# Twelve phases to a unit by a table, and the maxima taken together one pair later

## The chip, the cores and the metric

The kernel runs on one core of a Trainium2 chip. A core has a matrix engine (TensorE, "PE" in the profile, with its weight loads shown apart as "PEld"), a vector engine (VectorE, "DVE"), an engine for elementwise functions (ScalarE, "ACT"), a general engine (GpSimd, "POOL") and an engine that here only issues transfers (SyncE, "SP"). Each takes its own instructions in order and waits on semaphores for the others. TensorE writes to PSUM, a buffer of eight banks of 2 KB per partition, from where VectorE and ScalarE read. The metric is the device time of one execution in microseconds.

## The reference

Four layers on `x` of 2048 rows and 576 columns, in the order A, B, A, B. Each is an attention block of 32 heads of width 18 behind a layer norm, with a residual:

```python
def _A_ref(x, wqkv, wo):                     # B: one k and one v shared by all heads
    q, k, v = ...                            # x @ wqkv, 32 heads of 18
    scores = jnp.einsum("bhqd,bhkd->bhqk", q, k) * (Dh ** -0.5)
    p = _softmax(scores, axis=-1)
    o = jnp.einsum("bhqk,bhkd->bhqd", p, v)
    return (...)(o, 0, 2, 1, 3).reshape(B, S, D) @ wo

x = x + _A_ref(_layernorm(x), A_wqkv, A_wo)  # then B, A, B in the same way
```

Everything is fp32. Softmax is over 2048 keys, for 32 heads times 2048 queries, in each layer.

## The kernel before

Heads are worked in pairs (`NPAIR` = 16), and queries in four quarters of 512. A **unit** is one pair of heads and one quarter of queries, `(p, u)`; there are 64 in a layer. Operands of head 0 of a pair lie on partitions 0 to 63 and those of head 1 on 64 to 127, so that a matmul of one head uses one half of TensorE's rows. A unit has three kinds of matmul:

- **Products for the maxima** (`max_mm`, "m", L506): 128 queries against 512 keys of one head; 32 to a unit. Two of them fill the two banks of a tile `psm` (two such tiles, four banks). VectorE reduces a full tile along the keys (`reduce_max`, L515). After 32 products `max_final` (L626) takes the maxima of the unit together and negates them; GpSimd splits them into a high and a low part (L139, L630). `max_store` (L635, L637) transposes them on VectorE and stores them to DRAM in four transfers; `max_rows` (L641) loads them as two rows of the query operand.
- **Products for the exps** (`exp_mm`, "e", L650): 128 keys against 512 queries of one head, with the negated maximum in the two added rows; 32 to a unit. Each goes to one of three banks, `pse`; ScalarE turns it into a tile `pt` of probabilities (L654).
- **Products with the values** (`pv_cols`, `pv_block`, L675): four `pt` tiles at a time, each with 19 columns of weights (18 values and a one that gives the sum), in four column groups of TensorE. They add up in one bank, `oacc`. 4096 columns to a unit, eight blocks of 512. When a unit's last block is done, ScalarE copies the bank (L681).

The products for the maxima run ahead of those for the exps by 56 (`4 * LEAD`), the value products follow the exps two phases later. GpSimd then sums the parts, inverts the sums and scales (`o_sum`, `l_inv`, `o_mul`), with transfers between. Such work is entered in a table by steps of four exps (`at`, `run_todo`), and `run_todo` emits what has come due at the beginning of a phase.

The order of the work on TensorE is written out. The loop at L764 runs **phases**: row products, m and e, in an order given by `ORDERS`, then a number of value columns. A unit has eleven phases. Those with an even number have two m and three e, those with an odd number four m and three e, the eleventh two of each. The heads of the m alternate with the phase, the exps come in a fixed order (two of head 0, two of head 1). Ten phases have 384 value columns, the eleventh 256:

```python
for kind, n in ORDERS[2 if k == 10 else k % 2]:
    if kind == "e":
        ...exp_mm(...)
    elif m_done[0] < 4 * ns:
        max_mm(n ^ k // 2 % 2, ...)
exps += 2 if k == 10 else 3
if phase >= 2:
    pv_cols(256 if k == 10 else 384)
```

In `max_mm`, the reduce of the unit's last pair is followed at once by `max_final`. When all m are done, the same loop goes on with the e and the value columns that are left. At the beginning of a layer, m products alone are woven into the projections (`max_pairs`).

Of the kernel before, what the change touches and what calls it, by code (L numbers as in the profile page):

```python
# [19 lines left out]
NCH = S // P  # L20
NPAIR = H // 2
# [21 lines left out]
STEPS = 8  # L43
LEAD = 14
# [14 lines left out]

ORDERS = ([("m", 1), ("e", 0), ("m", 1), ("e", 1), ("e", 2)],
          [("m", 0), ("m", 1), ("e", 1), ("e", 0), ("m", 0), ("m", 1), ("e", 2)],
          [("m", 1), ("e", 0), ("m", 1), ("e", 1)])


@with_exitstack
def tile_kernel(ctx: ExitStack, tc: tile.TileContext, A_x, A_wqkv, A_wo, B_x, B_wq, B_wk, B_wv, B_wo, out):
# [53 lines left out]
    def mtile2(name):  # L123
        return psum.tile([P, 2, 512], F32, tag="m", bufs=2, name=name)
# [7 lines left out]
    def ptile(name, shape=(P, 512), dt=F32):  # L132
        return pool.tile(list(shape), dt, tag="p", bufs=15, name=name)

    def copy(eng, dst, src):
        if eng is nc.scalar:
            eng.activation(dst, src, AF.Copy)  # L137
        else:
            eng.tensor_scalar(dst, src, 1.0, 0.0, op0=OP.mult, op1=OP.add)  # L139
# [194 lines left out]
    def out_proj(last):  # L334

        for c in range(NCH):
            tt = c // 2
            if c == 1:
                out_rows(2)
            if c % 2 and tt + 3 < 8:  # L340
                out_rows(tt + 3)
            if c >= OUT_AHEAD:
                run_tail(TAIL)
            out_w(c)
            if c % 2 == 0 and tt + 1 < 8:
                out_t(tt + 1, nc.scalar)
            if last:
                nc.sync.dma_start(y_out[c * P:(c + 1) * P, :], xo[:, c])
            yield c
        assert not tail and not ors  # L350
# [4 lines left out]
    for layer in range(4):  # L355
# [124 lines left out]
        def ops(p):  # L480
            return big[:, q_slot(p)], big[:, k_slot(p)]

        m_open, m_next, m_done, m_count = [], [0, 0], [0], {}

        m_first = [] if is_a else ([(0, i // 2, i % 2) for i in range(8)] + [(1, i // 2, i % 2) for i in range(4)] +
                                   [(0, i, 2) for i in range(4)] + [(1, i // 2, i % 2) for i in range(4, 6)] +
                                   [(0, i, 3) for i in range(4)] + [(1, i // 2, i % 2) for i in range(6, 8)] +
                                   [(1, i, 2) for i in range(4)] + [(1, i, 3) for i in range(4)])

        def max_mm(a, slot):  # L490

            i = m_next[a]
            p, u = divmod(i // 16, 4)
            if i < len(m_first):
                u, qc, kb = m_first[i]
            else:
                qc, kb = i // 2 % 4, i // 8 % 2 * 2 + i % 2
            q, k = ops(p)
            if (p, u) not in mxs:
                mxs[p, u] = pool.tile([P, 32], F32, name="mx")  # L500
            if m_done[0] % 2 == 0:
                m_open.append((mtile2("psm"), []))
            ps, rows = m_open[0]
            b = 64 * a
            c0 = u * 512 + qc * P
            nc.tensor.matmul(ps[:, slot], q[b:b + KM, c0:c0 + P], k[b:b + KM, kb * 512:(kb + 1) * 512],  # L506
                             start=True, stop=True)
            rows.append((p, u, 16 * a + 4 * qc + kb))
            m_next[a] += 1
            m_done[0] += 1  # L510
            if m_done[0] % 2 == 0:
                m_open.pop()
                (p, u, r0), (p1, u1, r1) = sorted(rows)
                assert (p, u) == (p1, u1)
                nc.vector.reduce_max(mxs[p, u][:, r0:r1 + 1:r1 - r0], ps, axis=AX.X)  # L515
                m_count[p, u] = m_count.get((p, u), 0) + 2
                if m_count[p, u] == 32:
                    max_final(p, u)

        def max_pairs():  # L520

            if is_a:
                run_todo(m_done[0] // 4)
            for a in (0, 1, 0, 1):
                max_mm(a, a)
            if not is_a and m_done[0] == 48:
                max_store(0, 0)
            elif not is_a and m_done[0] == 52:
                max_rows(0, 0)
# [94 lines left out]
        def max_final(p, u):  # L624
            neg = pool.tile([P, 8], F32, name="neg")
            nc.vector.tensor_reduce(neg, mxs.pop((p, u)).rearrange("p (b k) -> p b k", k=4), axis=AX.X, op=OP.max,  # L626
                                    negate=True)
            hl = nms[p, u] = hls[(4 * p + u) % 2]
            copy(nc.gpsimd, hl[:, 0:8], neg)
            nc.gpsimd.tensor_tensor(hl[:, 8:16], neg, hl.bitcast(F32)[:, 0:8], op=OP.subtract)  # L630

        def max_store(p, u):

            tr = pool.tile([P, 32], F32, name="tr")
            nc.vector.transpose(tr, nms.pop((p, u)).bitcast(F32))  # L635
            for b in range(4):
                nc.sync.dma_start(m_d[u].rearrange("j a q (b i) -> b (j a q) i", b=4)[b], tr[32 * b:32 * b + 16, :])  # L637

        def max_rows(p, u):
            for a in range(2):  # L640
                nc.sync.dma_start(big_f[64 * a + KM:64 * a + KE, q_slot(p), u * 512:(u + 1) * 512],  # L641
                                  m_d[u][:, a].rearrange("j q p -> j (q p)"))

        def exp_mm(p, u, i, tail):

            a, kc = (i // 2) % 2, i // 4 * 2 + i % 2
            q, k = ops(p)
            e = (mtile if tail and i % 2 else etile)("pse")
            r = 64 * a
            nc.tensor.matmul(e, k[r:r + KE, kc * P:(kc + 1) * P], q[r:r + KE, u * 512:(u + 1) * 512],  # L650
                             start=True, stop=True)

            pt = pts[p, u, i] = ptile("pt")
            nc.scalar.activation(pt, e, AF.Exp, scale=SCALE)  # L654

        turn, pv_at = [0], [0]

        def pv_cols(cols):

            while cols:  # L660
                n, c0 = divmod(pv_at[0], 512)
                w = min(cols, 512 - c0)
                pv_block(n, c0, c0 + w)
                pv_at[0] += w
                cols -= w

        def pv_block(n, c0, c1):

            p, u, i = *divmod(n // STEPS, 4), n % STEPS * 4
            cs = slice(c0, c1)  # L670
            turn[0] += 1
            for i in range(i, i + 4) if turn[0] % 2 else range(i + 3, i - 1, -1):
                a, kc = (i // 2) % 2, i // 4 * 2 + i % 2
                j = 64 * a + 32 * (kc % 2)
                nc.tensor.matmul(oacc[j:j + DH + 1, cs], v_of(kc)[:, 2 * p + a if is_a else 0, :], pts[p, u, i][:, cs],  # L675
                                 start=kc < 2 and c0 == 0, stop=kc >= 14 and c1 == 512)
                if c1 == 512:
                    pts.pop((p, u, i))
            if c1 == 512 and i // 4 == STEPS - 1:
                oc = ocs[p, u] = ptile("oc")  # L680
                nc.scalar.activation(oc, oacc, AF.Copy)  # L681
# [38 lines left out]
        def at(b, f, *args):  # L720
            todo.setdefault(b, []).append((f, args))

        ns = STEPS * 4 * NPAIR
        for p in range(NPAIR):
            for u in range(4):
                b = STEPS * (4 * p + u) + STEPS - 1
# [20 lines left out]
        def run_todo(st):  # L747
            for n in sorted(n for n in todo if n <= st):
                for f, args in todo.pop(n):
                    f(*args)  # L750
# [9 lines left out]
                woven(max_pairs, 3, 8)  # L760
            f(*args)
        assert not weave["left"] and m_done[0] == 4 * LEAD
        exps = 0
        for phase in range(11 * 4 * NPAIR):  # L764
            k = phase % 11
            run_todo(LEAD + exps // 4)
            for kind, n in ORDERS[2 if k == 10 else k % 2]:
                if kind == "e":
                    n += exps
                    exp_mm(*divmod(n // 4 // STEPS, 4), n % (4 * STEPS), m_done[0] >= 4 * ns)  # L770
                elif m_done[0] < 4 * ns:
                    max_mm(n ^ k // 2 % 2, m_done[0] % 2 if k % 2 == 0 else n ^ k // 2 % 2)
            exps += 2 if k == 10 else 3
            if phase >= 2:
                pv_cols(256 if k == 10 else 384)
        outs = out_proj(layer == 3)
        for st in range(ns, ns + L_AT + 1):
            run_todo(LEAD + st)
            if st < ns + OUT_AHEAD:
                next(outs)  # L780
                pv_cols(256 * (1 + st - ns))
        tail = [todo.pop(n, []) for n in range(ns + LEAD + L_AT + 1, ns + LEAD + O_AT)]
        assert not todo, todo

# [30 lines left out]
```

## Time and profile before

| | |
|---|---|
| median of three runs | 5806.96 us (5803.63 to 5808.14) |
| profiled execution | 5805.73 us, its span 5803.9 us |
| granted TensorE clock in it, mean | 0.997 |
| PE busy | 5767.2 us (99%) |
| DVE busy | 5170.2 us (89%) |
| ACT busy | 4605.2 us (79%) |
| POOL busy | 1718.2 us (30%) |
| mean DMA | 48 GB/s |

An engine's busy time is the union of its instructions' spans. Matmuls are pipelined and their ends are modelled, so 99% for PE does not say that the array is always fed: a wait of less than a matmul's tail does not show as idle time. What PE waited for is read on the row of its weight loads, and the length of a piece of work from the starts of its matmuls. In a group's line, the numbers after the bar are the busy time in us and the mean length of one in ns, and after the second bar the idle time just before them and what ended it. In a line of the timeline, the first number is the start and the second the length, both in us.

### The profile page before, as it was taken

How to read it: one execution, taken by the hardware profiler on the slowest of the kernel's cores; microseconds unless marked ns; L12 is line 12 of the kernel's file. 1: busy time of each engine (PE TensorE's matmuls, PEld its weight loads, DVE VectorE, ACT ScalarE, POOL GpSimd, SP SyncE). 2: the span in 40 equal slices, each digit the busy share in tenths (PEclk: the TensorE clock that was granted, in tenths of full speed). 3: DMA queues.
4: the chain of work that ended last, by engine and by line, in shares of the span. 5: the costliest groups of instructions: out<-in, count | busy, mean ns of one | idle time of the engine just before them, and what ended most of it. 6: DMA issues, size and time to landing. Idle time of an engine off the chain costs nothing.

```text
span 5803.9 us, 132703 instructions
## 1 busy us (share of the span) xinstructions
PE 5767.2 (99%) x53756; PEld 2906.5 (50%) x53756; DVE 5170.2 (89%) x5336; ACT 4605.2 (79%) x8872; POOL 1718.2 (30%) x2207
## 2 busy tenths in 40 slices
PE   9999999999999999999999999999999999999999
PEld 7644444444844444444685444444448444444446
DVE  4799999998699999999647999999977999999995
ACT  2588888888378888888625888888882888888885
POOL 2133232323233232323311423232332332323232
PEclk9999999999999999999999999999999999999999
DMA  5311111110420000000243111111114100010002
GB/s 195 110 46 31 36 31 35 32 32 21 127 65 23 22 22 20 20 22 24 59 166 93 40 35 32 35 32 35 29 35 128 49 22 23 22 23 19 23 13 77
DMA packets 250305, 276.40 MB, mean 48 GB/s; under 512 B 131732, under 2 KB 171924, under 8 KB 239972
## 3 DMA queue, kind: packets, MB, share of 16 engines
q1 hardware_dynamic: 249692, 267.92, 16.7%
q8 instruction: 422, 6.91, 0.5%
q14 instruction: 191, 1.56, 0.1%
HBM read 151.24 MB, written 112.56 MB: 45 GB/s over the span
## 4 chain that ended last, share of the span: by engine, by line
PE 97%; DVE 1%; DMA 1%; POOL 1%; ACT 0%; SPq 0%; issue 0%; POOLq 0%; ACTq 0%; DVEq 0%
PE oacc L675 36%; PE psm L506 31%; PE pse L650 17%; PE psn L215 6%; PE psq L374 6%; DVE mx L515 1%; PE ps L207 0%; DMA raw<-in_B_wk_dram 0%; ACT pt L654 0%; DMA big<-m_d 0%; POOL big L162 0%; PE oacc L208 0%; SPq L151 0%; POOL os L689 0%; POOL os L711 0%
## 5 line engine op out<-in xcount | busy, mean ns | idle before, releaser
L515 DVE TENSOR_REDUCE mx<-psm 128x2 f32<-128x1024 f32 x4096 | 4768.8, 1217 | 168.3 <-PE psm L506 133.6
L654 ACT ACTIVATE pt<-pse 128x512 f32<-128x512 f32 x8192 | 4314.4, 602 | 550.3 <-PE pse L650 368.2
L650 PE MATMUL pse<-big 64*128 64x512 f32 x8192 | 2448.6, 418 | 10.3 <-DMA big<-m_d 8.8
L506 PE MATMUL psm<-big 62*128 62x512 f32 x8192 | 2285.6, 452 | 5.7 <-DVE mx L515 5.6
L675 PE MATMUL oacc<-pt,vbuf 128*19 128x384 f32 (+1 forms) x24560 | 1756.0, 384 | 1.9 <-ACT oc L681 1.9
L506 PEld LDWEIGHTS psm<-big 62*128 62x128 f32 x8192 | 925.0, 184 | 1468.0 <-DVE mx L515 923.8
L650 PEld LDWEIGHTS pse<-big 64*128 64x128 f32 x8192 | 1188.3, 185 | 293.0 <-ACT pt L654 193.1
L675 PEld LDWEIGHTS oacc<-pt,vbuf 128*19 128x19 f32 x24560 | 501.0, 97 | 772.0 <-issue 594.3
L139 POOL TENSOR_SCALAR hl<-neg 128x8 fp32r<-128x8 f32 x256 | 50.9, 199 | 2681.0 <-DVE neg L626 2681.0
L675 PE MATMUL oacc<-pt,vy 128*19 128x256 f32 x8176 | 593.2, 385 | 0.0
L698 POOL TENSOR_TENSOR rl<-lt,mone 128x8 f32<-128x8 f32 x256 | 423.4, 1654 | 573.2 <-DMA lt<-os 573.1
L139 POOL TENSOR_SCALAR os<-oc 32x512 f32<-32x512 f32 x512 | 314.6, 614 | 129.6 <-ACT oc L681 87.7
L711 POOL TENSOR_TENSOR os<-os,rb 96x512 f32<-96x512 f32 x256 | 329.2, 1286 | 20.9 <-DMA rb<-r_d 20.1
L689 POOL TENSOR_TENSOR os<-os,oc 96x512 f32<-96x512 f32 x256 | 326.4, 1275 | 21.4
L382 ACT ACTIVATE ev<-psq 128x512 fp32r<-128x512 f32 (+1 forms) x112 | 67.0, 598 | 321.2 <-PE psq L374 240.4
L215 PE MATMUL psn<-wsm,xx 128*128 128x288 f32 x2240 | 307.4, 296 | 0.0
L215 PEld LDWEIGHTS psn<-wsm,xx 128*128 128x128 f32 x2240 | 298.6, 188 | 10.8 <-issue 8.0
L675 PEld LDWEIGHTS oacc<-pt,vy 128*19 128x19 f32 x8176 | 177.2, 98 | 251.1 <-issue 202.5
L388 DVE TENSOR_TENSOR ev<-psq,ev 128x512 fp32r<-128x512 f32 (+1 forms) x84 | 58.0, 691 | 218.6 <-ACT ev L382 202.9
L374 PE MATMUL psq<-yx,big 128*128 128x512 f32 (+2 forms) x812 | 199.6, 399 | 2.1 <-ACT big L137 0.8
L374 PE MATMUL psq<-xx,big 128*128 128x512 f32 (+1 forms) x784 | 194.5, 398 | 0.0
L681 ACT ACTIVATE oc<-oacc 128x512 f32<-128x512 f32 x256 | 157.7, 616 | 28.7 <-PE oacc L675 28.7
(66 smaller groups left out, 1370.9 us busy)
## 6 DMA issues: line engine op xcount, KB each, us to landing
big<-qk_d SPq DMA_DIRECT2D x180, 432.0 KB
qk_d<-ev SPq DMA_DIRECT2D x96, 512.0 KB
qk_d<-ev SPq DMA_DIRECT2D x120, 256.0 KB
rb<-r_d SPq DMA_DIRECT2D x512, 36.0 KB
o_d<-os SPq DMA_DIRECT2D x512, 36.0 KB
m_d<-tr SPq DMA_DIRECT2D x1024, 2.0 KB
o<-o_d SPq DMA_DIRECT2D x64, 256.0 KB
big<-m_d SPq DMA_DIRECT2D x512, 4.0 KB
```

The source lines that it names most:

```text
L139: eng.tensor_scalar(dst, src, 1.0, 0.0, op0=OP.mult, op1=OP.add)
L215: nc.tensor.matmul(ps, lhs[:, xc, :], wsm[:, wc, h * 288:(h + 1) * 288], start=i == 0, stop=i == len(TERMS) - 1)
L374: nc.tensor.matmul(ps[:n].rearrange("p (u t) -> p u t", u=2)[:, us], w[:, wc, :n], xts[T][:, us, xc, :], start=j == 0, stop=j == len(TERMS ...
L506: nc.tensor.matmul(ps[:, slot], q[b:b + KM, c0:c0 + P], k[b:b + KM, kb * 512:(kb + 1) * 512], start=True, stop=True)
L515: nc.vector.reduce_max(mxs[p, u][:, r0:r1 + 1:r1 - r0], ps, axis=AX.X)
L650: nc.tensor.matmul(e, k[r:r + KE, kc * P:(kc + 1) * P], q[r:r + KE, u * 512:(u + 1) * 512], start=True, stop=True)
L654: nc.scalar.activation(pt, e, AF.Exp, scale=SCALE)
L675: nc.tensor.matmul(oacc[j:j + DH + 1, cs], v_of(kc)[:, 2 * p + a if is_a else 0, :], pts[p, u, i][:, cs], start=kc < 2 and c0 == 0, stop=k ...
L681: nc.scalar.activation(oc, oacc, AF.Copy)
L689: nc.gpsimd.tensor_tensor(t[:96], t[:96], oc[:96], op=OP.add)
L698: nc.gpsimd.tensor_tensor(rl, lts.pop((p, u)), mone, op=OP.pow)
L711: nc.gpsimd.tensor_tensor(t[:96], t[:96], rb[:96], op=OP.mult)
```

## The change

`ORDERS` gives way to a table `UNIT` of twelve phases. Each has its own order of row products, written with kind and head, and its own number of value columns. The sums over a unit stay: 32 m (16 of each head), 32 e (16 of each head), 4096 columns. The exps of each head now count by themselves (`e_next`), so their order across heads follows the table. The loop ends when all m are done; a second loop takes the remaining e by threes with 384 columns each.

The heads of all m (`m_heads`) and the bank of its tile that each uses (`m_banks`) are worked out ahead. Whichever of a pair comes first in the row of maxima gets the first bank.

`max_final` is no longer called behind the reduce that completes a unit, but behind the next one (`m_full`).

```diff
-ORDERS = ([("m", 1), ("e", 0), ("m", 1), ("e", 1), ("e", 2)],
-          [("m", 0), ("m", 1), ("e", 1), ("e", 0), ("m", 0), ("m", 1), ("e", 2)],
-          [("m", 1), ("e", 0), ("m", 1), ("e", 1)])
+UNIT = [("m0 m1 e0 e0 e1 m0 m1", 384), ("e0 m1 m0 e1 e0", 352), ("m0 m1 e1 e0 e1 m0 m1", 320), ("m1 e0 e1 m0", 256),
+        ("m1 e0 m1 e0 e1", 416), ("e1 m0 m0 e1 m1 e0", 416), ("e1 m0 m1 e0 e1 m0", 384), ("e0 e1 m0 m1 e0", 256),
+        ("m1 e0 m0 e1", 128), ("e1 m0 m1 e0", 192), ("e1 m0 m1 e0", 416), ("m0 m1 e1 e0 e1 m1 m0", 576)]
+UNIT = [([(o[0], int(o[1])) for o in rows.split()], cols) for rows, cols in UNIT]
...
+        m_heads = ([0, 1] * (2 * LEAD) + [g for rows, _ in UNIT for kind, g in rows if kind == "m"] * (4 * NPAIR))[:4 * ns]
+        m_banks, n = [], [0, 0]
+        for i in range(0, 4 * ns, 2):
+            at_ = []
+            for a in m_heads[i:i + 2]:
+                p, u, qc, kb = max_place(a, n[a])
+                at_.append((p, u, 16 * a + 4 * qc + kb))
+                n[a] += 1
+            m_banks += [0, 1] if at_[0] < at_[1] else [1, 0]
...
                 nc.vector.reduce_max(mxs[p, u][:, r0:r1 + 1:r1 - r0], ps, axis=AX.X)
+                while m_full:
+                    max_final(*m_full.pop())
                 m_count[p, u] = m_count.get((p, u), 0) + 2
                 if m_count[p, u] == 32:
-                    max_final(p, u)
+                    m_full.append((p, u))
...
+        e_next = [0, 0]
+
+        def exp_next(a):
+            pu, kc = divmod(e_next[a], NCH)
+            exp_mm(*divmod(pu, 4), kc // 2 * 4 + 2 * a + kc % 2, m_done[0] >= 4 * ns)
+            e_next[a] += 1
+
+        phase = 0
+        while m_done[0] < 4 * ns:
+            rows, cols = UNIT[phase % len(UNIT)]
+            run_todo(LEAD + sum(e_next) // 4)
+            for kind, a in rows:
                 if kind == "e":
-                    n += exps
-                    exp_mm(*divmod(n // 4 // STEPS, 4), n % (4 * STEPS), m_done[0] >= 4 * ns)
+                    exp_next(a)
                 elif m_done[0] < 4 * ns:
-                    max_mm(n ^ k // 2 % 2, m_done[0] % 2 if k % 2 == 0 else n ^ k // 2 % 2)
-            exps += 2 if k == 10 else 3
+                    max_mm()
             if phase >= 2:
-                pv_cols(256 if k == 10 else 384)
+                pv_cols(cols)
+            phase += 1
...
+        while sum(e_next) < 4 * ns:
+            run_todo(LEAD + sum(e_next) // 4)
+            for _ in range(min(3, 4 * ns - sum(e_next))):
+                exp_next(int(e_next[0] > e_next[1]))
+            pv_cols(384)
```

Behind the loops, `pv_cols(256 * (1 + st - ns))` becomes `pv_cols(512 * ns - pv_at[0] - (0 if st > ns else 512))`: the columns that are left but 512, then 512. `max_pairs` calls `max_final` for what is complete at its end.

More of the change, by code (lines that the diff above doesn't have):

```diff
@@ L481, in ops @@
             return big[:, q_slot(p)], big[:, k_slot(p)]
-        m_open, m_next, m_done, m_count = [], [0, 0], [0], {}
+        m_open, m_next, m_done, m_count, m_full = [], [0, 0], [0], {}, []
         m_first = [] if is_a else ([(0, i // 2, i % 2) for i in range(8)] + [(1, i // 2, i % 2) for i in range(4)] +
@@ L488, in tile_kernel, with max_place, max_mm @@
                                    [(1, i, 2) for i in range(4)] + [(1, i, 3) for i in range(4)])
-        def max_mm(a, slot):
-            i = m_next[a]
+        def max_place(a, i):
             p, u = divmod(i // 16, 4)
             if i < len(m_first):
-                u, qc, kb = m_first[i]
-            else:
-                qc, kb = i // 2 % 4, i // 8 % 2 * 2 + i % 2
+                return (0, *m_first[i])
+            return p, u, i // 2 % 4, i // 8 % 2 * 2 + i % 2
+        ns = STEPS * 4 * NPAIR
+        m_heads = ([0, 1] * (2 * LEAD) + [g for rows, _ in UNIT for kind, g in rows if kind == "m"] * (4 * NPAIR))[:4 * ns]
[7 more added lines that the diff above has]
+            m_banks += [0, 1] if at_[0] < at_[1] else [1, 0]
+        def max_mm():
+            a, slot = m_heads[m_done[0]], m_banks[m_done[0]]
+            p, u, qc, kb = max_place(a, m_next[a])
             q, k = ops(p)
@@ L523, in max_pairs @@
                 run_todo(m_done[0] // 4)
-            for a in (0, 1, 0, 1):
-                max_mm(a, a)
+            for _ in range(4):
+                max_mm()
+            while m_full:
+                max_final(*m_full.pop())
             if not is_a and m_done[0] == 48:
@@ L721, in at @@
             todo.setdefault(b, []).append((f, args))
-        ns = STEPS * 4 * NPAIR
         for p in range(NPAIR):
@@ L762, in tile_kernel @@
         assert not weave["left"] and m_done[0] == 4 * LEAD
[L763 to L767, printed above, removed]
+        e_next = [0, 0]
[8 more added lines that the diff above has]
+            for kind, a in rows:
                 if kind == "e":
-                    n += exps
-                    exp_mm(*divmod(n // 4 // STEPS, 4), n % (4 * STEPS), m_done[0] >= 4 * ns)
+                    exp_next(a)
                 elif m_done[0] < 4 * ns:
-                    max_mm(n ^ k // 2 % 2, m_done[0] % 2 if k % 2 == 0 else n ^ k // 2 % 2)
-            exps += 2 if k == 10 else 3
+                    max_mm()
             if phase >= 2:
-                pv_cols(256 if k == 10 else 384)
+                pv_cols(cols)
+            phase += 1
+        while m_full:
+            max_final(*m_full.pop())
+        while sum(e_next) < 4 * ns:
[3 more added lines that the diff above has]
+            pv_cols(384)
         outs = out_proj(layer == 3)
@@ L780, in tile_kernel @@
                 next(outs)
-                pv_cols(256 * (1 + st - ns))
+                pv_cols(512 * ns - pv_at[0] - (0 if st > ns else 512))
         tail = [todo.pop(n, []) for n in range(ns + LEAD + L_AT + 1, ns + LEAD + O_AT)]
```

## The prediction

> **What bounds the kernel now.** I read the page first: busy shares, the chain that ended last, the costly groups.
>
> ```profile
> PE 5767.2 (99%) x53756; PEld 2906.5 (50%) x53756; DVE 5170.2 (89%) x5336; ACT 4605.2 (79%) x8872; POOL 1718.2 (30%) x2207
> ...
> PE 97%; DVE 1%; DMA 1%; POOL 1%; ACT 0%; SPq 0%; issue 0%; POOLq 0%; ACTq 0%; DVEq 0%
> PE oacc L675 36%; PE psm L506 31%; PE pse L650 17%; PE psn L215 6%; PE psq L374 6%; DVE mx L515 1%; PE ps L207 0%; DMA raw<-in_B_wk_dram 0%; ACT pt L654 0%; DMA big<-m_d 0%; POOL big L162 0%; PE oacc L208 0%; SPq L151 0%; POOL os L689 0%; POOL os L711 0%
> ...
> L515 DVE TENSOR_REDUCE mx<-psm 128x2 f32<-128x1024 f32 x4096 | 4768.8, 1217 | 168.3 <-PE psm L506 133.6
> L654 ACT ACTIVATE pt<-pse 128x512 f32<-128x512 f32 x8192 | 4314.4, 602 | 550.3 <-PE pse L650 368.2
> ...
> L506 PEld LDWEIGHTS psm<-big 62*128 62x128 f32 x8192 | 925.0, 184 | 1468.0 <-DVE mx L515 923.8
> ```
>
> The chain is TensorE: value products (L675), row products for the maxima (L506), row products for the exps (L650). But TensorE's loads wait for the reduce of the maxima, so VectorE is close behind. The unit's length comes from one copy of the accumulator per unit, by its source line inside layer 1:
>
> ```profile
> L681 ACT ACTIVATE oc<-oacc x58: 614/617/617, 1659.2 to 2762.4; 128x512 f32<-128x512 f32 x58
> ```
>
> 57 gaps in 1103.2 us: 19.354 us per unit. The maxima lead by 56 products, so 62 units per layer run with everything, 248 in four layers: 4800 of the 5804 us. The change acts there. TensorE's order of time inside one unit (start, length, what):
>
> ```profile
> 805.59 0.50 PE L506 MATMUL psm<-big 62*128 62x512 f32 x1
> ...
> 806.57 0.84 PE L675 MATMUL oacc<-pt,vbuf 128*19 128x384 f32 x8
> ...
> 810.94 0.50 PE L506 MATMUL psm<-big 62*128 62x512 f32 x2
> ...
> 812.17 0.84 PE L675 MATMUL oacc<-pt,vbuf 128*19 128x384 f32 x8
> ...
> 814.60 0.50 PE L506 MATMUL psm<-big 62*128 62x512 f32 x2
> ...
> 815.72 0.42 PE L675 MATMUL oacc<-pt,vbuf 128*19 128x128 f32 x8
> ...
> 819.34 0.84 PE L675 MATMUL oacc<-pt,vy 128*19 128x384 f32 x8
> 820.11 0.50 PE L506 MATMUL psm<-big 62*128 62x512 f32 x1
> ...
> 820.77 0.63 PE L675 MATMUL oacc<-pt,vy 128*19 128x256 f32 x8
> ...
> 821.33 0.50 PE L506 MATMUL psm<-big 62*128 62x512 f32 x1
> ```
>
> Two products of different heads use different row halves and start together; I call such a pair, or one product without a partner, a slot. From 814.60 four slots take 1.12 us until the value columns start; from 820.11 two take 0.66: 0.23 a slot, 0.20 ahead of the first and behind the last. 384 value columns take 0.77 (819.34 to 820.11), 256 take 0.56 (820.77 to 821.33): 0.217 per 128 and 0.125 fixed. So a phase costs 0.325, plus 0.23 a slot, plus its columns. Before: 37 slots (five phases of 3, five of 4, one of 2), 11 phases, 4096 columns: 8.51 + 3.575 + 6.94 = 19.03. The remaining 0.33 of the 19.354 is waiting. Two waits are seen whole: 3 slots from 805.59 last 0.98 instead of 0.89, and 4 slots from 810.94 last 1.23 instead of 1.12. The weight loads say why:
>
> ```profile
> 806.57 0.14 PEld L675 LDWEIGHTS oacc<-pt,vbuf 128*19 128x19 f32 x8 [0.30 <-ACT oc L681]
> ...
> 811.51 0.19 PEld L506 LDWEIGHTS psm<-big 62*128 62x128 f32 x2 [0.28 <-DVE mx L515]
> ```
>
> VectorE and ScalarE in the same unit:
>
> ```profile
> 804.23 3.49 DVE L515 TENSOR_REDUCE mx<-psm 128x2 f32<-128x1024 f32 x3 [0.21 <-PE psm L506]
> 807.75 0.19 DVE L626 TENSOR_REDUCE neg<-mx 128x8 f32<-128x32 f32 x1
> 807.88 2.36 DVE L515 TENSOR_REDUCE mx<-psm 128x2 f32<-128x1024 f32 x2
> 810.15 0.20 DVE L635 STREAM_TRANSPOSE tr<-hl 128x32 f32<-128x32 f32 x1
> 810.28 4.69 DVE L515 TENSOR_REDUCE mx<-psm 128x2 f32<-128x1024 f32 x4
> ```
>
> ```profile
> 804.45 1.58 ACT L654 ACTIVATE pt<-pse 128x512 f32<-128x512 f32 x3 [0.32 <-PE pse L650]
> 805.90 0.62 ACT L681 ACTIVATE oc<-oacc 128x512 f32<-128x512 f32 x1
> ```
>
> Three reduces take 3.49 and two 2.36: one every 1.13 us, though each lasts 1.22. The last reduce ahead of 807.75 began at 806.50 (its end 807.72 less 1.22); the next could have begun at 807.63, but begins at 807.88: the unit's maxima (L626) cost VectorE 0.25, because they read what that reduce writes and wait for its end. The transpose, behind a reduce that it does not read, costs 0.13. VectorE needs 16 x 1.13 + 0.25 + 0.13 = 18.5 of 19.35. An exp follows the last by 0.49 (1.58 less 0.60, halved).
>
> **The change, part by part.** Orders and columns. By pairs of unlike heads in the order written, the twelve phases have 4, 3, 4, 2, 3, 3, 3, 3, 2, 2, 2 and 4 slots: 35. Without waits: 8.05 + 12 x 0.325 = 3.90 + 6.94 = 18.89. That is 0.46 gained by two slots and 0.325 lost by one more phase.
>
> Maxima one pair later. L626 then stands behind a reduce that it does not read, as the transpose does: 0.13 for 0.25, and VectorE's need falls to 18.37. Behind it go two GpSimd operations, the transpose, four stores and two loads per unit. Their order on GpSimd's and SP's queues does not change; the transpose keeps its two reduces of distance from L626. On VectorE it falls 8.8 us into the unit (walk below), 10.7 ahead of the next unit's first exp product; before, at 810.15, 11.2 ahead of the one at 821.33. So the rows' way through DRAM has 0.4 us less:
>
> ```profile
> 2012.06 1.69 SPq L637 DMA_DIRECT2D m_d<-tr  x4
> ...
> 2015.99 0.52 SPq L641 DMA_DIRECT2D big<-m_d  x2
> ```
>
> ```profile
> 2023.04 0.73 PE L650 MATMUL pse<-big 64*128 64x512 f32 x2
> ```
>
> The reload is issued 3.9 us after the first store, once the stores have landed; from there to the product that needs it are 7.05 us, and 6.6 then. I cost the move at nothing; were that cover gone, each microsecond too late would cost 248. Where weight loads hold up SP's queue it is gone already, as in this stall in layer 0; it stays, give or take 2 us.
>
> ```profile
> 1349.96 0.76 PE L650 MATMUL pse<-big 64*128 64x512 f32 x1 [3.53 <-DMA big<-m_d]
> ```
>
> Waits. I walk through the unit with steps from the rows: the reduce starts 0.55 after the load of a first-slot pair of maxima products (803.68 to 804.23; 0.23 more per later slot) or 1.13 after the last one; its two banks are free 0.05 after its end (810.28 + 1.18, load at 811.51); an exp starts 0.44 after its slot's matmuls or 0.49 after the last exp, and frees its bank 0.65 after its start; a load goes out one slot ahead, so 0.12 of its lateness is free.
>
> ```
> phase  start  slots columns  wait   for
>  1      0.00    4     384    0.04   reduce that began 0.54 before the unit
>  2      1.94    3     352    -
>  3      3.55    4     320    0.10   third exp product: the exp begun at 3.46
>  4      5.44    2     256    -
>  5      6.66    3     416    0.01   exp bank
>  6      8.40    3     416    0.05   reduce begun at 7.64
>  7     10.17    3     384    0.06   reduce begun at 9.17
>  8     11.89    3     256    -
>  9     13.34    2     128    0.01   exp bank
> 10     14.36    2     192    -
> 11     15.47    2     416    -
> 12     16.97    4     576    -
> ```
>
> The unit's copy of the accumulator falls between phases 2 and 3, and four slots (1.12) now lie ahead of the next value columns, which hides it; before it lay ahead of three and cost 0.09. VectorE idles 0.11, 0.28 and 0.40 us ahead of its fourth, eighth and ninth reduce. Waits: 0.27, with roundings 0.28; the unit is 18.89 + 0.28 = 19.17. The same walk gives 19.38 for the unit before, 0.03 over the measured one.
>
> Short value segments. The columns cut into 18 pieces instead of 16, two of them of 64 and 32 columns. Their passes (two per piece, 54 and 27 ns by the rate) may be held to a smallest step. The nearest row is the transposes with 18 moving columns:
>
> ```profile
> 1534.42 0.32 PEld L417 LDWEIGHTS psv<-ident,vt 18*128 18x128 f32 x4 [0.17 <-issue]
> L417 PEld LDWEIGHTS psv<-ident,vt 18*128 18x128 f32 x32 | 2.6, 136 | 1.7 <-issue 1.4 <-PE ps L207 0.3
> ```
>
> Four loads in 0.32, each 0.136: a step of 62 ns, with weights of 128 columns. Ends: nothing, and 2 x (62 - 27) + 2 x (62 - 54) = 0.09 us a unit. With 19-column weights I take 0.01. The Trainium skill (TensorEngine Tiling (Array Packing), Instruction Overhead) has about 60 cycles as the overhead of each matmul, so that fewer columns win nothing; its estimate is 25 ns, below both passes, so by the page the term is zero and the sum 2 us lower. No run here shows a matmul that short in this form.
>
> Layer ends: the 55 exps behind the last maxima take 19 phases before and after, columns moved but not changed in number: nothing.
>
> Sum: 19.354 - 19.17 - 0.01 = 0.174 us x 248 = 43 us. The profiled execution took 5805.73 (span 5803.9 and 1.8 around it), 1.2 below the median 5806.96; I predict 5763 against that median.
>
> **Rivals.** One: L626's place gains nothing, since VectorE lets one instruction end before the next. Then the walk with 0.25 in its new place gives 19.31 less the 0.03: 0.07 x 248 = 18 us, 5789. Against it: reduces of 1.22 start every 1.13. [...] Chance 0.10.
>
> Two: short passes at their upper end: 0.184 - 0.09 = 0.09 x 248, 5784. Chance 0.08.
>
> Three: a lone product inside a phase (phase 1 between its second and third slot, phase 12 in its third) delays the pair behind it; in the kernel before, the lone product always is the phase's last. Price: the load not hidden, 0.11 (the step from 803.68 to 803.79 below), at two places: 0.22, making 19.40, 11 us slower or no change (5818). For it: no row shows the case. Against: with pairs, loads for the same row half follow each other too, and a slot still takes 0.23. Chance 0.06.
>
> ```profile
> 803.68 0.18 PEld L506 LDWEIGHTS psm<-big 62*128 62x128 f32 x2 [0.21 <-issue]
> 803.79 0.19 PEld L650 LDWEIGHTS pse<-big 64*128 64x128 f32 x2
> ```
>
> Four, on the other side: exps bind. Phases 7 to 10 hold ten exps in 1.72 + 1.45 + 1.02 + 1.11 = 5.3 us, because their value columns are few. At a step of 0.49 that fits; it decides from 0.53 on. Eight exps in 4.50 us elsewhere (0.56 a step, with small gaps) speak for it, the row of three against it. At 0.56: 5.6 - 5.3 = 0.3 more, 19.47, 0.12 x 248 = 29 us slower, 5836. Chance 0.12, with all that lengthens VectorE's step, since it is then within 4% of binding.
>
> **How the numbers follow.** The forecast has 0.64. Faster: 0.64 + 0.10 + 0.08 = 0.82; within 0.2% (some 12 us, about what a measurement of this kernel can tell from no change) 0.06; slower 0.12. The forecast's own range is 5745 to 5780 (the walk misses the unit before by 0.03, thus 7 us, and each step by up to 0.06). The range to hold 8 in 10 reaches from 5730 (the waits of 0.28 a fifth gone besides) to 5820, which leaves out the fourth rival.
>
> **What would show it.** Copies of the accumulator 19.17 apart; L626's successor costing 0.13 between reduces; no wait for the copy at the value columns; waits for the reduce in phases 1, 6 and 7; four slots still 1.12. Wrong, if exps follow each other without gaps from phase 7 to 10 and row products wait for them, if the pair behind a lone product starts late, or if loads wait for the stored maxima in every unit.

## The result

The kernel after takes 5764.46 us against 5806.16 us before, medians of six runs each, in turn on one chip: 41.7 us less. The ratio, of the means, is 0.9933 (95% interval 0.9923 to 0.9943); four of the six runs of after lie between 5763.7 and 5765.1 us, two at 5771 and 5773. The forecast was 5763.

The page of the kernel after, the lines that answer to those shown of before:

```profile
PE 5726.2 (99%) x57884; PEld 2924.8 (51%) x57884; DVE 5127.3 (89%) x5336; ACT 4580.3 (79%) x8872; POOL 1718.2 (30%) x2207
...
L531 DVE TENSOR_REDUCE mx<-psm 128x2 f32<-128x1024 f32 x4096 | 4736.3, 1218 | 179.0 <-PE psm L522 157.3
...
L670 PE MATMUL pse<-big 64*128 64x512 f32 x8192 | 2494.3, 433 | 10.0 <-DMA big<-m_d 8.0
...
L670 PEld LDWEIGHTS pse<-big 64*128 64x128 f32 x8192 | 1226.5, 185 | 865.5 <-ACT pt L674 683.0
L522 PEld LDWEIGHTS psm<-big 62*128 62x128 f32 x8192 | 1055.4, 185 | 809.0 <-DVE mx L531 637.2
```

Of the kernel before, the lines for these readings are in the prediction, but for that of the exps' loads:

```profile
L650 PEld LDWEIGHTS pse<-big 64*128 64x128 f32 x8192 | 1188.3, 185 | 293.0 <-ACT pt L654 193.1
```

No share moves by more than a point. The busy times of PE, DVE and ACT fall by 41, 43 and 25 us. The idle time of loads put down to VectorE falls from 923.8 to 637.2 us, and that put down to ScalarE at the exps' products rises from 193.1 to 683.0. That is idle time of the load path, most of it hidden behind value columns; the unit tells what it is worth. The copies of the accumulator, by their source line, in the same layer as before:

```profile
L701 ACT ACTIVATE oc<-oacc x58: 617/618/621, 1668.3 to 2761.4; 128x512 f32<-128x512 f32 x58
```

57 gaps in 1093.1 us: 19.177 us, where 19.17 and 0.01 for short pieces were worked out. Times 248 units the 0.177 are 43.9 us; the times differ by 41.7.

TensorE in order of time (start, length, what), the first line of each phase's row products and of its value columns, from phase 12 to phase 7 of the next unit:

```profile
2007.31 0.50 PE L522 MATMUL psm<-big 62*128 62x512 f32 x2
...
2008.45 1.17 PE L695 MATMUL oacc<-pt,vbuf 128*19 128x288 f32 x16
2009.55 0.51 PE L522 MATMUL psm<-big 62*128 62x512 f32 x2
...
2010.71 0.85 PE L695 MATMUL oacc<-pt,vbuf 128*19 128x224 f32 x16
2011.49 0.49 PE L670 MATMUL pse<-big 64*128 64x512 f32 x1
...
2012.38 0.79 PE L695 MATMUL oacc<-pt,vbuf 128*19 128x352 f32 x8
2013.10 0.50 PE L522 MATMUL psm<-big 62*128 62x512 f32 x2
...
2014.32 0.73 PE L695 MATMUL oacc<-pt,vbuf 128*19 128x320 f32 x8
2014.98 0.50 PE L522 MATMUL psm<-big 62*128 62x512 f32 x1
...
2015.65 0.63 PE L695 MATMUL oacc<-pt,vbuf 128*19 128x192 f32 x16
2016.21 0.50 PE L522 MATMUL psm<-big 62*128 62x512 f32 x1
...
2017.12 0.90 PE L695 MATMUL oacc<-pt,vbuf 128*19 128x416 f32 x8
2017.94 0.49 PE L670 MATMUL pse<-big 64*128 64x512 f32 x1
...
2018.83 0.90 PE L695 MATMUL oacc<-pt,vbuf 128*19 128x32 f32 x16
2019.66 0.49 PE L670 MATMUL pse<-big 64*128 64x512 f32 x1
...
2020.66 0.63 PE L695 MATMUL oacc<-pt,vbuf 128*19 128x128 f32 x12
```

In this unit the row products last 1.14 us in phase 12 (four slots, 1.12 without a wait), 1.16 in phase 1, 0.89 in phase 2, 1.22 in phase 3, 0.67 in phase 4, 0.91 in 5, 0.89 in 6 and 1.00 in 7. The walk had 1.12, 1.16, 0.89, 1.22, 0.66, 0.90, 0.94 and 0.95. The value columns keep their rate: 576 take 1.10, 352 take 0.72.

VectorE around the maxima of a unit:

```profile
2001.08 14.92 DVE L531 TENSOR_REDUCE mx<-psm 128x2 f32<-128x1024 f32 x13 [0.33 <-PE psm L522]
2015.91 0.18 DVE L646 TENSOR_REDUCE neg<-mx 128x8 f32<-128x32 f32 x1
2016.01 2.35 DVE L531 TENSOR_REDUCE mx<-psm 128x2 f32<-128x1024 f32 x2
2018.27 0.20 DVE L655 STREAM_TRANSPOSE tr<-hl 128x32 f32<-128x32 f32 x1
```

The thirteenth reduce ends at 2016.00, so it began at 14.78 and the next could have begun at 15.91. It begins at 16.01: taking the maxima together now costs 0.10 us, where it cost 0.25. The operation (L646) begins 0.09 us before the reduce in front of it ends.

### The profile page after: what moved, and what is told of

Same layout as the page of the kernel before. It is cut to its first block, busy times and chain, and to the rows that moved or that the text cites. A ratio compares the mean times of both kernels' runs of the same rounds, so it can differ in the third digit from the quotient of the medians.

```text
span 5763.3 us, 141224 instructions
## 1 busy us (share of the span) xinstructions
PE 5726.2 (99%) x57884; PEld 2924.8 (51%) x57884; DVE 5127.3 (89%) x5336; ACT 4580.3 (79%) x8872; POOL 1718.2 (30%) x2207
## 5 line engine op out<-in xcount | busy, mean ns | idle before, releaser
L522 PE MATMUL psm<-big 62*128 62x512 f32 x8192 | 2540.4, 453 | 4.1 <-DVE mx L531 4.0
L670 PE MATMUL pse<-big 64*128 64x512 f32 x8192 | 2494.3, 433 | 10.0 <-DMA big<-m_d 8.0
L695 PE MATMUL oacc<-pt,vbuf 128*19 128x320 f32 (+5 forms) x27664 | 1783.3, 360 | 5.2 <-ACT oc L701 5.2
L670 PEld LDWEIGHTS pse<-big 64*128 64x128 f32 x8192 | 1226.5, 185 | 865.5 <-ACT pt L674 683.0
L522 PEld LDWEIGHTS psm<-big 62*128 62x128 f32 x8192 | 1055.4, 185 | 809.0 <-DVE mx L531 637.2
L695 PEld LDWEIGHTS oacc<-pt,vbuf 128*19 128x19 f32 x27664 | 537.8, 98 | 779.4 <-issue 598.7
L695 PE MATMUL oacc<-pt,vy 128*19 128x192 f32 (+2 forms) x9200 | 594.9, 361 | 0.0
L695 PEld LDWEIGHTS oacc<-pt,vy 128*19 128x19 f32 x9200 | 196.6, 98 | 273.0 <-issue 213.6
```

## The experiments

Two theories were set against each other. **Theory 1**, hand-overs: the unit is TensorE's sum (slots, phases, columns) plus the waits that come out when each product, reduce and exp is walked through in order. **Theory 2**, sums: VectorE and ScalarE have slack, so only slots and phases count.

### The table without the move of the maxima

```diff
                 nc.vector.reduce_max(mxs[p, u][:, r0:r1 + 1:r1 - r0], ps, axis=AX.X)
-                while m_full:
-                    max_final(*m_full.pop())
                 m_count[p, u] = m_count.get((p, u), 0) + 2
                 if m_count[p, u] == 32:
-                    m_full.append((p, u))
+                    max_final(p, u)
```

> The table of twelve phases as in the kernel after, but the unit's maxima are taken together right behind the reduce that completes them, as before. Theory 1 (hand-overs: a unit is TensorE's sum plus its waits for VectorE and ScalarE, phase by phase, by the walk of the prediction): the 0.25 us on VectorE come back and shift the reduces of phases 5 to 8, the unit is 19.28 us, the time about 5788 us (0.997 of before). Theory 2 (sums: the gain is two slots less, 0.46, against one phase more, 0.325, so 0.135 us a unit, and VectorE has slack): 5773 us. If the move of the maxima gains nothing: 5764, as after.

Measured: 5792.72 us, ratio 0.9979 (0.9970 to 0.9989). A unit is 19.287 us (55 gaps):

```profile
L699 ACT ACTIVATE oc<-oacc x56: 617/619/622, 1694.0 to 2754.8; 128x512 f32<-128x512 f32 x56
```

Its VectorE at the maxima:

```profile
1999.27 4.74 DVE L531 TENSOR_REDUCE mx<-psm 128x2 f32<-128x1024 f32 x4
2004.05 0.19 DVE L644 TENSOR_REDUCE neg<-mx 128x8 f32<-128x32 f32 x1
2004.15 3.48 DVE L531 TENSOR_REDUCE mx<-psm 128x2 f32<-128x1024 f32 x3
```

The fourth reduce began at 2002.79, the next could have at 2003.92 and begins at 2004.15: 0.23. The operation between (L644) begins at 2004.05, 0.04 behind the end of the reduce whose output it reads. So 0.13 us more on VectorE than in the kernel after is 0.11 more in the unit. The table alone brings 0.067 of the 0.177.

### The move of the maxima without the table

```diff
...
+                while m_full:
+                    max_final(*m_full.pop())
                 m_count[p, u] = m_count.get((p, u), 0) + 2
                 if m_count[p, u] == 32:
-                    max_final(p, u)
+                    m_full.append((p, u))
+                if m_done[0] == 4 * ns:
+                    while m_full:
+                        max_final(*m_full.pop())
...
```

> The kernel before, with its eleven phases, and only the unit's maxima taken together one pair later (right away behind the layer's last pair). Theory 1 (hand-overs): VectorE has 0.12 us less to do, but the maxima and the transpose now stand on both sides of the same reduce, just ahead of the one whose bank the sixth phase waits for; that wait grows from 0.12 to 0.26 us, the unit is 19.49 us and the time 5840 us, slower than before. Theory 2 (sums): VectorE's saving is worth up to 0.12 us a unit, 5776 to 5806 us, not slower.

Measured: 5827.83 us, ratio 1.0037 (1.0022 to 1.0051): slower, with less work on VectorE (busy 5158.7 us against 5170.2), though 12 us less slow than worked out. The copies, VectorE, then the unit's sixth phase on TensorE and the load of its second pair:

```profile
L688 ACT ACTIVATE oc<-oacc x56: 618/619/619, 1683.8 to 2754.4; 128x512 f32<-128x512 f32 x56
```

```profile
2016.72 1.23 DVE L515 TENSOR_REDUCE mx<-psm 128x2 f32<-128x1024 f32 x1 [0.18 <-PE psm L506]
2017.86 0.17 DVE L633 TENSOR_REDUCE neg<-mx 128x8 f32<-128x32 f32 x1
2017.95 1.22 DVE L515 TENSOR_REDUCE mx<-psm 128x2 f32<-128x1024 f32 x1
2019.08 0.20 DVE L642 STREAM_TRANSPOSE tr<-hl 128x32 f32<-128x32 f32 x1
2019.21 3.48 DVE L515 TENSOR_REDUCE mx<-psm 128x2 f32<-128x1024 f32 x3
```

```profile
2019.78 0.50 PE L506 MATMUL psm<-big 62*128 62x512 f32 x2
...
2021.11 0.84 PE L682 MATMUL oacc<-pt,vbuf 128*19 128x384 f32 x8
```

```profile
2020.44 0.19 PEld L506 LDWEIGHTS psm<-big 62*128 62x128 f32 x2 [0.36 <-DVE mx L515]
```

The maxima cost VectorE some 0.1 us here too, and the transpose 0.13, one reduce later. In the kernel before, the 0.25 lay ahead of the reduce that stands first here. Without it VectorE has to wait for TensorE there (0.18 us idle), so little is saved; and the 0.10 now lies behind that wait, just ahead of the reduce at 2019.21, whose bank the sixth phase needs. Its row products take 1.33 us instead of 1.23, and the unit is 19.465 (1070.6 us over 55 gaps), 0.11 more. The two parts of the change are worth -0.07 and +0.11 us alone and -0.18 together: their effects don't add.

### Value columns in proportion to the exps

```diff
-UNIT = [([(o[0], int(o[1])) for o in rows.split()], cols) for rows, cols in UNIT]
+UNIT = [([(o[0], int(o[1])) for o in rows.split()], 128 * rows.count("e")) for rows, _ in UNIT]
```

> The kernel after, but each phase has 128 value columns for each of its exps (384 or 256) in place of its own number; orders, slots, phases and the place of the maxima are those of after. Theory 1 (hand-overs): the four-slot phases 12 and 1 follow on two-slot phases with full columns, their second pair waits for the reduce (0.3 to 0.4 us more in phase 1, 0.1 in phase 12, some in phase 7), the unit is 19.62 us, the time about 5871 us, slower than before. Theory 2 (sums): slots, phases and columns have the same sum, so 5764 us as after.

Measured: 5878.28 us, ratio 1.0124 (1.0109 to 1.0139). Slots, phases and columns are those of the kernel after, and the time is 74 us above before. A unit is 19.637 us (54 gaps), 0.46 more than in the kernel after:

```profile
L701 ACT ACTIVATE oc<-oacc x55: 619/620/621, 1698.9 to 2759.3; 128x512 f32<-128x512 f32 x55
```

Phases 12 and 1, and the load of phase 1's second pair:

```profile
2006.76 0.50 PE L522 MATMUL psm<-big 62*128 62x512 f32 x2
...
2008.02 0.85 PE L695 MATMUL oacc<-pt,vbuf 128*19 128x128 f32 x16
2008.80 0.50 PE L522 MATMUL psm<-big 62*128 62x512 f32 x2
...
2010.28 0.85 PE L695 MATMUL oacc<-pt,vbuf 128*19 128x256 f32 x16
```

```profile
2009.85 0.19 PEld L522 LDWEIGHTS psm<-big 62*128 62x128 f32 x2 [0.51 <-DVE mx L531]
```

Phase 12 takes 1.26 us for its row products and phase 1 takes 1.48, against 1.14 and 1.16, which is 0.44 of the 0.46: two phases with four maxima products each come after one another with only 384 columns between and 256 ahead of them, and TensorE waits for the reduce. In the table as changed, 576 columns lie between and 416 ahead. Most of the columns for these two places come from the phases 8, 9 and 10, which have two maxima products each.

### Half the reduce, in both kernels

The reduce reads the first 256 of each 512 scores, and half the keys are left out of the maxima.

```diff
-                nc.vector.reduce_max(mxs[p, u][:, r0:r1 + 1:r1 - r0], ps, axis=AX.X)
+                nc.vector.reduce_max(mxs[p, u][:, r0:r1 + 1:r1 - r0], ps[:, :, :256], axis=AX.X)
```

> The kernel before, but the reduce reads only the first 256 of each 512 scores, so half the keys are left out of the maxima (the softmax still holds, with another maximum). A reduce then takes about 0.6 us instead of 1.13. Theory 1 (hand-overs): the waits for VectorE go, those for the exps' three banks and for the accumulator's copy stay: 19.22 us a unit, 5772 us. Rival (VectorE is what fills a unit's 0.33 us of waiting): the unit falls to TensorE's sum of 19.03, 5726 us.

> The kernel after with the same cut: the reduce reads 256 of each 512 scores, half the keys are left out of the maxima. Theory 1: waits for exp banks stay, 19.06 us a unit, 5733 us, so the two kernels are 0.16 us a unit apart, nearly as far as with the whole reduce. Rival: the unit falls to TensorE's sum of 18.89, 5692 us.

Measured: 5773.74 us (0.9943, 0.9929 to 0.9956) and 5735.00 us (0.9876, 0.9861 to 0.9891). VectorE's busy share falls from 89% to 54% and 56%. The copies, first those of the kernel before with half the reduce:

```profile
L681 ACT ACTIVATE oc<-oacc x57: 618/619/619, 1688.9 to 2768.0; 128x512 f32<-128x512 f32 x57
```

```profile
L701 ACT ACTIVATE oc<-oacc x57: 617/617/618, 1694.0 to 2763.2; 128x512 f32<-128x512 f32 x57
```

19.270 and 19.093 us a unit. Half the reduce is worth 0.08 us in each kernel, and the rest of what the sum without waits leaves (0.24 before, 0.20 after) stays. The two kernels are 0.177 us a unit apart, as with the whole reduce, and 38.7 us in time. So with far less work on VectorE the change is worth nearly the same: 0.135 us of slots against a phase, and 0.04 of waits that half the reduce does not remove. That the place of the maxima and the numbers of columns keep VectorE from taking it back is what the table alone (0.11 us lost) and the columns by exps (0.46 lost) show.

### Two other tables

Both have 36 slots and twelve phases, and orders and columns for which the walk finds almost no wait. The first begins and ends like this:

```diff
-UNIT = [("m0 m1 e0 e0 e1 m0 m1", 384), ("e0 m1 m0 e1 e0", 352), ("m0 m1 e1 e0 e1 m0 m1", 320), ("m1 e0 e1 m0", 256),
...
+UNIT = [("e1 m1 m0 e0 e1 m1 m0", 352), ("e0 m0 e1 e0 m1", 448), ("m1 m0 e1 e0 e1 m0 m1", 448), ("m0 e1 e0 m0 e1", 288),
...
+        ("m1 e0 m0 e1", 288), ("e1 e0 m1 m0 e1", 352), ("e0 m0 m1 m1 e0 m0 e1", 352), ("e1 e0 m1 m1 e0", 448)]
...
```

In both, the number of columns left at a layer's end is also kept from falling below zero.

> Another table of twelve phases, with 36 slots instead of 35, orders and columns set by the walk so that loads wait as little as possible: value columns of 448 behind some four-slot phases, 128 ahead of others. Maxima one pair later, as in after. Theory 1 (hand-overs): one slot more is 0.23 us, and nearly all of the waiting of 0.28 us goes; the unit is 19.13 to 19.14 us, 5755 us, 10 us under after. Theory 2 (sums): one slot more costs 0.23 us a unit, 5821 us.

> A third table with twelve phases and 36 slots, other orders and columns (128 to 448) with the same sum of the walk. Theory 1: 19.13 to 19.14 us a unit, 5755 us, as the second table. Theory 2: 5821 us.

Measured: 5781.51 us (0.9956, 0.9944 to 0.9968) and 5774.28 us (0.9942, 0.9929 to 0.9954). Copies, of the first table and the second:

```profile
L701 ACT ACTIVATE oc<-oacc x57: 616/617/619, 1691.1 to 2767.9; 128x512 f32<-128x512 f32 x57
```

```profile
L700 ACT ACTIVATE oc<-oacc x57: 603/604/607, 1688.9 to 2764.8; 128x512 f32<-128x512 f32 x57
```

19.229 and 19.212 us. These tables, with a slot more and other orders and columns, cost 0.03 to 0.05 us a unit and not 0.23: most of the slot is won back from waits. Theory 2 is out by 40 us and more. But the walk was too low by 0.07 to 0.09 as well: it promised a table better than the changed one, and there is none here. On the mean over layer 1, no one wait stands out in either: the row products of every phase last up to 0.02 longer than slots of 0.23 give (four slots 1.13 to 1.14 instead of 1.12), which adds up to 0.11 and 0.09. Whether these hundredths are short waits or slots read too short is not shown. For tables this close to each other the walk, right to 0.05 elsewhere, can't choose.

## Why the prediction was right

By its steps, with the unit in us:

| kernel | worked out | measured |
|---|---|---|
| before | 19.38 (walk) | 19.354 |
| after | 19.18 | 19.177 |
| table alone | 19.28 | 19.287 |
| move alone | 19.49 | 19.465 |
| columns by exps | 19.62 | 19.637 |
| half reduce, before | 19.22 | 19.270 |
| half reduce, after | 19.06 | 19.093 |
| other tables | 19.13 to 19.14 | 19.229, 19.212 |

**Slots and phases.** A slot of 0.23 and a phase of 0.325 hold to about 0.01: the phases without waits last 0.66 to 0.67 us with two slots and 0.90 with three, where the sum has 0.66 and 0.89. The half reduce leaves 0.177 between the kernels, a little more than the 0.135 of slots and phase.

**The maxima one pair later.** The step was right and its size a little short: 0.10 us on VectorE where 0.13 was taken from the transpose. The first rival, by which the place gains nothing, had 5789; the table alone, without the move, took 5793, so the move is worth some 28 us with this table, and the rival falls. What decides is what the operation reads: behind a reduce that it does not read it costs 0.10 and begins before that reduce ends (kernel after), behind the one that it reads it costs 0.23 and begins after its end (table alone). The Trainium skill (VectorE: DVE Perf Modes, The DRAIN you can't avoid) has the next operation wait until the pipe is empty, but adds that one that is not held starts earlier; the trace agrees with the earlier start, as reduces of 1.22 us follow each other every 1.13.

**Waits.** 0.28 us were worked out, and the unit less its sum leaves 0.29. By place, in the unit shown: phase 1 has 0.04 as worked out, phase 3 has 0.10 as worked out, phase 7 about 0.1 where 0.06 was expected, and phase 6 has none where 0.05 was expected. Rows of phases 1 and 3 name the reasons:

```profile
2010.27 0.19 PEld L522 LDWEIGHTS psm<-big 62*128 62x128 f32 x2 [0.20 <-DVE mx L531]
...
2013.65 0.18 PEld L670 LDWEIGHTS pse<-big 64*128 64x128 f32 x1 [0.25 <-ACT pt L674]
...
2014.32 0.14 PEld L695 LDWEIGHTS oacc<-pt,vbuf 128*19 128x19 f32 x8 [0.37 <-ACT oc L701]
```

```profile
2013.47 0.62 ACT L701 ACTIVATE oc<-oacc 128x512 f32<-128x512 f32 x1
```

```profile
2018.71 1.23 DVE L531 TENSOR_REDUCE mx<-psm 128x2 f32<-128x1024 f32 x1 [0.24 <-PE psm L522]
```

The load at 2013.65 is phase 3's third exp product, waiting for its bank. The one at 2014.32 names the copy of the accumulator, but that had ended at 2014.09, 0.23 earlier; in the kernel before, the load followed 0.05 behind the copy's end. So the copy is hidden, as the prediction said, though the row still names it. The misses of phases 6 and 7 belong together. The reduce that phase 6 was to wait for begins 7.59 us into the unit (2016.01 and one step of 1.13, from 2009.55) instead of 7.64, because the maxima cost less, so phase 6 doesn't wait and phase 7 starts 0.06 earlier. The reduce at 2018.71, 9.16 into the unit where the walk had 9.17, then holds phase 7 up by that much more.

**Short value segments.** 0.01 was taken, of up to 0.09. Measured: 416 columns as 32 and 384 (from 2018.83) take 0.83 us and in one piece (from 2017.12) 0.82; 256 as 192 and 64 (from 2015.65) take 0.56, as in one piece before. The second rival falls: the term is at most 0.01, with pieces as short as the change has.

**The other rivals.** A lone product inside a phase would have cost 0.11 at phases 1 and 12; they take 1.16 and 1.14, and the first has 0.04 of that from the reduce. Exps that bind in phases 7 to 10 would have cost 0.3; the measured unit leaves no room for it. Half of what was named as its sign did appear:

```profile
2002.77 4.66 ACT L674 ACTIVATE pt<-pse 128x512 f32<-128x512 f32 x9 [0.15 <-PE pse L670]
```

From phase 8 on nine exps follow each other every 0.51 us with hardly a gap, close to the step of 0.49. But the row products of the phases 9 and 10 last 0.67 us on the mean over layer 1, as two slots do without a wait, so ScalarE is close to its limit there and does not hold TensorE up. The way of the maxima through DRAM stayed covered: exps' products waited 8.0 us for it over the whole kernel, 8.8 before.

**Layer ends** were costed at nothing, which was wrong by some 4 us. The last three copies of a layer lie 39.5 to 39.8 us apart before; after, they lie 40.2 apart in the first three layers and 41.7 in the last. The last layer, before and after:

```profile
L681 ACT ACTIVATE oc<-oacc x3: 599/616/617, 5708.7 to 5748.2; 128x512 f32<-128x512 f32 x3
```

```profile
L701 ACT ACTIVATE oc<-oacc x3: 597/619/682, 5665.9 to 5707.6; 128x512 f32<-128x512 f32 x3
```

The 43.9 us of the units less these 4 are close to the 40.6 by which the two profiled spans differ; what in a layer's end takes longer, and the rest, was not taken apart.

**Where luck helped.** The mechanism came out as forecast, but a hit to 2 us is better than the working could promise. The walk was 0.03 too high for the kernel before, and the forecast left that in while the first rival's price had it taken off; treated alike, the forecast would have been 5756, or the rival 5796. The small misses (a gain of 0.177 where 0.174 was worked out, layer ends that cost 4 us) also went against each other. Two sums are rough without effect: VectorE's need after the move adds up to 18.34 and not 18.37, and the starts in the walk end at 19.19 where its waits give 19.17.

## What to carry to other kernels

Where several engines are close to binding, if only in stretches, a sum over one engine can rank two orders wrongly: with the same slots, phases and columns the time moved by 2%, and each half of this change alone gave a third of the gain or a loss. Walk each hand-over through one period with the profile's own steps (when a buffer comes free, when a load may go out), check the walk on the kernel at hand, and trust it no further than it misses there; for tables chosen by the walk itself it missed by more (0.07 to 0.09). Place the work that no neighbour needs at once behind something that it does not read, and give the long stretches of one engine to the places where another is behind.

## What was not expected

That the move of the maxima by itself makes the kernel slower by 0.4% while VectorE has less to do is not in the prediction; the walk gave it after the result, before that run. That a smallest piece of 32 columns (27 ns a pass by the rate) costs nothing measurable, with four column groups in turn, no row of before had shown. And two tables with one slot more came within 10 to 17 us of the changed one.
